# Attention, Mish MLP and bilinear MLP in one kernel: weight conversion in stages, fp32 attention results, a third transpose bank

## The chip, the cores and the metric

The kernel runs on one core of a Trainium2 chip. The metric is the device time of one execution in microseconds (us). Engines are named as the profile names them: PE is TensorE (PEld its weight loads), DVE is VectorE, ACT is ScalarE, POOL is GpSimd, SP is SyncE, whose queue issues the DMAs.

## What is computed

Attention over 4 batches and 8 heads of 576 tokens and 64 dimensions, in which each row keeps only scores within tau of its maximum; then two MLPs over the 2304 tokens.

```python
scores = scale * np.matmul(q, k.transpose(0, 1, 3, 2))
thresh = np.max(scores, axis=-1, keepdims=True) - tau
scores = np.where(scores >= thresh, scores, -1000000000.0)
...
attn = np.exp(scores)
attn = attn / (np.sum(attn, axis=-1, keepdims=True) + 1e-09)
return np.matmul(attn, v).astype(np.float32)
...
h = x @ w_in
sp = np.where(h > 20.0, h, np.log1p(np.exp(np.minimum(h, 20.0))))
g = h * np.tanh(sp)
return (g @ w_out).astype(np.float32)
...
a = x @ w_a
b = x @ w_b
return (a * b @ w_out).astype(np.float32)
```

The model is 512 wide, the first MLP 2048, the second 1536. The weights arrive as 64-bit floats.

## The kernel before

**Attention.** Two heads make a pair, 16 pairs in all. A pair is five units: four of 128 queries for both heads (c = 0 to 3) and one that holds the last 64 queries of both (c = 4, half the columns for DVE and ACT). The loop `for n in range(len(units) + 3)` (L379) takes 80 units through a pipeline of four steps, and the order in which it calls its helpers is, engine by engine, the order in which the engines run (`manual_schedule`). In step n:

- unit n: DVE copies its scores out of PSUM with the row minimum of the negated scores (`least`, L247, one instruction a head); POOL adds the bar (`bars`); ACT takes the exponentials (`expo`, L260).
- unit n-1 (`prev`): DVE masks and sums (`mask`, L265, one a head), POOL adds 1e-9 to the sums (`sums`, L272).
- unit n-2 (`mid`): DVE inverts the sums, POOL spreads the reciprocals into a 128x128 block of `pm` (`spread`, L280), PE transposes `pm` in three parts of 4, 4 and 2 blocks (`turned`, L290) into tiles `tp` of the pool `ps_t`, which has two banks, and ACT copies each part to `pt` (`back`).
- unit n-3 (`old`): PE multiplies with v (`weighted`, L310) into a tile `po` of the pool `ps_o`, which has two banks; DVE multiplies with the transposed reciprocals (`divide`, L324).
- unit n+1: PE computes its scores (`scores`, L233), into the one pair of `sp` tiles there is.

After a pair's last unit, `send` (L335) splits the pair's result into a high and a low fp32r part (ACT, POOL) and writes both to DRAM (`xd`).

**Weights.** PE works in fp32r, so each weight is split in a high and a low part, and each product is three matmuls (`mm3`). A block is a 128x512 piece of a weight. `weight` (L73) converts one in eight stages, each on its engine; from a 64-bit block, the words are put together as: ACT `u` (L94), DVE `a` (L96, L101), POOL add (L105), ACT square (L107), DVE `f` (L109), ACT high part (L111), low part (L113) on the engine that the caller names. `convert(eng)` (L347) goes one stage on where the first block's next stage is on `eng`; the attention loop calls it for ACT, DVE, DVE and POOL in each step from n = 2 on, so a block takes two or three steps, and up to five stages of one block follow each other in one step. All 16 blocks of the first half of w_in and w_out are converted in attention, with the low part on POOL.

**MLPs.** `pipeline` (L460) runs three phases over six tiles of 384 tokens: m1(0) and m1(1), each with half of the 2048 hidden units in eight blocks f, and m2 with twelve. Here the compiler's scheduler orders each engine's work, in the program's order of priority. `load_x` (L144) loads the high and low parts of a tile. The other blocks are converted during the matmuls, with the low part on DVE. PE starts on them while the last attention units are in flight.

Of the kernel before, what the change touches and what calls it, by code (L numbers as in the profile page):

```python
# [21 lines left out]
CC = DM // 128  # L22
# [3 lines left out]
T0 = 2  # L26
# [8 lines left out]
def tile_attn_mish_bilinear(ctx, tc, qd, kd, vd, vd2, tau, w_in, w_out, w_a, w_b, w_out2, out):  # L35
# [23 lines left out]
    xd = [  # L59
        [[dram.tile([128, S], F32, name=f"xd{i}{c}_{b}") for b in range(B)] for c in range(CC)] for i in range(2)  # L60
    ]
# [81 lines left out]

    def load_x(nm, t):  # L144
        x = x_tiles(nm)
        for c in range(CC):
            for i in range(2):
                done = 0
                while done < NM:
                    b, t0 = divmod(t * NM + done, S)  # L150
                    n = min(NM - done, S - t0)
                    nc.sync.dma_start(out=f32(x[c][i][:, done:done + n]), in_=xd[i][c][b][:, t0:t0 + n])
                    done += n
        return x
# [22 lines left out]
    with late_pools:  # L177
        at = late_pools.enter_context(tc.tile_pool(name="at", bufs=1, side="right"))
        ps_t = late_pools.enter_context(tc.tile_pool(name="ps_t", bufs=2, space=PSUM, side="right"))
        ps_o = late_pools.enter_context(tc.tile_pool(name="ps_o", bufs=2, space=PSUM, side="right"))  # L180
# [36 lines left out]
        ph = at.tile([128, 6, 128], F32, name="ph")  # L217

        def new_unit(n):
            pi, c = units[n]  # L220
            nm = f"{pi}_{c}"
            st = lambda s: at.tile([128, 2], F32, tag=s, name=s + nm, bufs=4)
            u = {s: st(s) for s in ("m", "te", "sm", "r")}
            h = 2 if c < 4 else 1
            u.update(pi=pi, c=c, nm=nm, h=h, po=None)
# [46 lines left out]
        def sums(u):  # L272
            n = u["h"]
            G.tensor_scalar(out=u["sm"][:, :n], in0=u["sm"][:, :n], scalar1=1e-9, scalar2=None, op0=ALU.add)
# [5 lines left out]
        def spread(u):  # L280

            if u["h"] == 1:
                G.tensor_copy(u["pm"][:, 5], u["r"][:, :1].to_broadcast([128, 128]))
            else:
                G.tensor_copy(
                    u["pm"][:, 9].rearrange("p (a d) -> p a d", a=2),
                    u["r"].unsqueeze(2).to_broadcast([128, 2, D]),
                )
# [21 lines left out]
        def weighted(u, v):  # L310

            c, pt = u["c"], u["pt"]
            u["po"] = po = ps_o.tile([128, 128], F32, tag="po", name="po" + u["nm"])
# [33 lines left out]
        def convert(eng):  # L347

            if not conv or ahead[0] is not eng:
                return  # L350
            try:
                ahead[0] = next(conv[0])
            except StopIteration:
                conv.pop(0)
                ahead.pop(0)
                if len(conv) > 1:
                    ahead.append(next(conv[1]))

        def attention():
# [7 lines left out]
            ahead.extend(next(g) for g in conv[:2])  # L367
            us = {0: new_unit(0)}
            scores(us[0], data[0])
            late = {}  # L370

            def turn(i):

                u = us[i]
                if u["h"] == 2:
                    return [lambda j=j, m=m: turned(u, j, m) for j, m in ((0, 4), (4, 4), (8, 2))]
                return [lambda j=j, m=m: turned(u, j, m) for j, m in ((0, 4), (4, 2))]

            for n in range(len(units) + 3):  # L379
# [12 lines left out]
                if mid:  # L392
                    parts = turn(n - 2)
                    backs = [part() for part in parts[:-1]]
# [8 lines left out]
                if u and u["h"] == 2:  # L403
                    expo(u, 1)
# [27 lines left out]
            while conv:  # L432
                convert(ahead[0])
# [63 lines left out]
    def m1(half):  # L497
        f0 = half * FC1 // 2

        def first(t, f, x):  # L500
# [4 lines left out]
            return mish(hp, nm)  # L505
# [11 lines left out]
        def after(t, f):  # L517
# [12 lines left out]
            start=lambda t: load_x(f"m{half}_{t}", t), finish=finish, after=after, skew=3,  # L530
# [78 lines left out]
```

## Time and profile before

| | us |
|---|---|
| median of three runs | 1218.99 (1218.48 to 1219.94) |
| the profiled execution's own time | 1222.38 |
| its span, first to last instruction | 1220.6 |
| attention alone: until the first MLP matmul | 354 |
| from there to the end of the span | 867 |

The span lies inside the profiled execution's own time; 1.8 us lie around it. In the views, "busy" is the time in which an engine had an instruction running. On the lines of the timeline, the bracket at the end is the idle time of the engine just before the instruction and what ended it.

### The profile page before, as it was taken

The numbers are of one execution on the slowest core, as the hardware profiler recorded it, in microseconds if no ns is written. First come the engines' busy times: TensorE is split into PE (matmuls) and PEld (weight loads), VectorE is DVE, ScalarE is ACT, GpSimd is POOL, SyncE is SP. The second block draws the span as 40 slices with busy tenths as digits, with TensorE's granted clock in tenths as the row PEclk, the third lists the DMA queues.
The fourth block names the chain that finished last, engine by engine and source line by source line (L and its number), as shares of the span: only waits on it lengthen the run. The fifth ranks groups of instructions, "written<-read, shape, count | busy, mean of one in ns | idle before, by whom it ended". The sixth has DMA issues, their size and how long they took to land.

```text
span 1220.6 us, 20246 instructions
## 1 busy us (share of the span) xinstructions
PE 1170.3 (96%) x7836; PEld 1083.1 (89%) x7836; DVE 585.0 (48%) x1300; ACT 537.0 (44%) x1031; POOL 255.9 (21%) x346
## 2 busy tenths in 40 slices
PE   8888888899999999999999999899999999999998
PEld 5665655677789999999999999899999999999998
DVE  5877778787866991177621138722112121121111
ACT  5777667687865762256522235522112121121211
POOL 2545445465533340022200002200000000000000
PEclk8989899899999999999999999999999999999999
DMA  4334533524304652146533215401001010010000
GB/s 174 119 128 154 175 112 130 181 89 141 120 22 159 214 168 92 53 155 207 190 104 99 83 51 180 151 1 52 1 1 53 1 52 1 1 52 1 26 2 26
DMA packets 75073, 113.53 MB, mean 93 GB/s; under 512 B 6752, under 2 KB 59104, under 8 KB 74976
## 3 DMA queue, kind: packets, MB, share of 16 engines
q1 hardware_dynamic: 74688, 111.93, 27.7%
q8 instruction: 62, 1.02, 0.3%
q10 hardware_dynamic: 288, 0.30, 0.1%
q14 instruction: 35, 0.29, 0.1%
HBM read 88.61 MB, written 23.59 MB: 92 GB/s over the span
## 4 chain that ended last, share of the span: by engine, by line
PE 81%; DVE 10%; ACT 4%; issue 2%; DMA 1%; POOL 1%; SPq 0%; ACTq 0%; DVEq 0%; POOLq 0%
PE acc L134 9%; PE acc L135 9%; PE acc L136 9%; PE po L318 5%; PE hm L134 5%; PE hm L135 5%; PE hm L136 5%; PE tp L303 5%; PE sp L243 4%; PE ha L134 4%; PE ha L135 4%; PE ha L136 4%; PE hb L134 4%; PE hb L136 4%; PE hb L135 4%; DVE s L251 3%
## 5 line engine op out<-in xcount | busy, mean ns | idle before, releaser
L541 DVE TENSOR_TENSOR s<-hb,s 128x384 f32<-128x384 f32 x72 | 40.1, 556 | 275.9 <-PE hb L136 275.9
L105 POOL TENSOR_TENSOR aw<-aw,uw 128x512 int32<-128x512 int32 x68 | 97.6, 1436 | 355.6 <-DVE aw L101 318.0
L173 DVE TENSOR_TENSOR glm<-hsm,ghm 128x384 fp32r<-128x384 f32 x96 | 78.7, 819 | 164.0 <-ACT ghm L172 163.7
L303 PE MATMUL tp<-ident,pm 128*128 128x128 f32 x640 | 105.6, 289 | 34.9 <-DVE pm L266 21.1
L303 PEld LDWEIGHTS tp<-ident,pm 128*128 128x128 f32 x640 | 71.8, 144 | 75.0 <-issue 31.2
L135 PE MATMUL hm<-xlm,w 128*128 128x384 f32 x384 | 129.2, 336 | 0.0
L306 ACT ACTIVATE pt<-tp 128x512 f32<-128x512 f32 (+1 forms) x192 | 98.8, 520 | 68.7 <-PE tp L303 66.4
L134 PE MATMUL hm<-xhm,w 128*128 128x384 f32 x384 | 128.9, 336 | 0.0
L136 PE MATMUL hm<-xhm,w 128*128 128x384 f32 x384 | 128.8, 335 | 0.0
L136 PE MATMUL acc<-ghm,w 128*128 128x384 f32 x384 | 128.7, 335 | 0.0
L135 PE MATMUL acc<-glm,w 128*128 128x384 f32 x384 | 128.7, 335 | 0.0
L134 PE MATMUL acc<-ghm,w 128*128 128x384 f32 x384 | 128.7, 335 | 0.0
L251 DVE TENSOR_SCALAR_CACHE_REDUCE s<-sp 128x576 f32<-128x576 f32 x144 | 103.9, 754 | 31.3 <-PE sp L243 22.9
L540 ACT ACTIVATE s<-ha 128x384 f32<-128x384 f32 x72 | 35.3, 490 | 187.1 <-PE ha L136 187.1
L171 ACT ACTIVATE hsm<-hm 128x384 f32<-128x384 f32 x96 | 46.7, 486 | 153.6 <-PE hm L136 153.3
L263 ACT ACTIVATE ex<-s,m 128x576 f32<-128x576 f32 x144 | 109.2, 769 | 8.3 <-DVE s L251 7.3
L266 DVE SCALAR_TENSOR_TENSOR pm<-s,te,ex 128x576 f32<-128x576 f32 x128 | 105.0, 857 | 0.0
L134 PE MATMUL acc<-gh,w 128*128 128x384 f32 x288 | 96.7, 337 | 4.2 <-DVE y L512 2.5
L135 PE MATMUL acc<-gl,w 128*128 128x384 f32 x288 | 97.1, 337 | 0.5 <-DVE gl L71 0.5
L134 PE MATMUL ha<-xhy,w 128*128 128x384 f32 x288 | 97.0, 337 | 0.0
L135 PE MATMUL ha<-xly,w 128*128 128x384 f32 x288 | 96.9, 336 | 0.0
L136 PE MATMUL ha<-xhy,w 128*128 128x384 f32 x288 | 96.8, 336 | 0.0
(80 smaller groups left out, 2482.3 us busy)
## 6 DMA issues: line engine op xcount, KB each, us to landing
raww<-w_out SPq DMA_DIRECT2D x28, 512.0 KB, 4.1
v<-vd SPq DMA_DIRECT2D x16, 576.0 KB, 4.3
raww<-w_in SPq DMA_DIRECT2D x16, 512.0 KB, 4.3
xhm<-xd SPq DMA_DIRECT2D x32, 192.0 KB, 4.0
xlm<-xd SPq DMA_DIRECT2D x32, 192.0 KB, 4.1
raww<-w_a SPq DMA_DIRECT2D x12, 512.0 KB, 3.6
raww<-w_b SPq DMA_DIRECT2D x12, 512.0 KB, 3.9
v<-vd SPq DMA_DIRECT2D x16, 320.0 KB, 4.7
```

Source lines behind the costliest of these rows:

```text
L105: G.tensor_tensor(out=a, in0=a, in1=u, op=ALU.add)
L134: PE.matmul(ps, wh, xh, start=start, stop=False)
L135: PE.matmul(ps, wh, xl, start=False, stop=False)
L136: PE.matmul(ps, wl, xh, start=False, stop=stop)
L173: V.tensor_tensor(out=g[1], in0=hs, in1=f32(g[0]), op=ALU.subtract)
L243: PE.matmul(sp[:, half, 0:288], d["qs"][r, cols], d["k"][r, keys], start=True, stop=True)
L251: V.tensor_scalar(out=u["s"][:, h].rearrange("p (a c) -> p a c", a=2), in0=u["sp"][h][:, :, 0:288], scalar1=1.0, scalar2=None, op0=ALU.mul ...
L263: A.activation(u["e"][:, h], u["s"][:, h], AF.Exp, bias=u["m"][:, h:h + 1], scale=-1.0)
L266: V.scalar_tensor_tensor(out=u["pm"].rearrange("p a c -> p (a c)")[:, h * S:(h + 1) * S], in0=u["s"][:, h], scalar=u["te"][:, h:h + 1], in ...
L303: PE.transpose(tp[:, i], pm[:, j0 + i], ident)
L306: A.activation(pt[:, j0:j0 + m], tp[:, :m], AF.Copy)
L318: PE.matmul(po[r], v[0][:, j + 4 * h, r], pt[:, j + 4 * h], start=j == 0, stop=j == 4)
```

## The change

- **Conversion.** `convert` no longer looks for an engine. It is called once a step, and a block goes on by one stage a step (the POOL add and the ACT square in one), so that what a stage reads was issued a step earlier. A new block starts every eight steps (`PACE`). Ten blocks (`EARLY` = 5, twice) are converted in attention, the low part on DVE; the other six of the first half in m1(0), tile 0.
- **Attention results** leave as one fp32 array `xd`; `load_x` loads that and splits it (ACT, DVE). The first tile is loaded and split during the last four pairs (`first_x`).
- **POOL** keeps `bars` and the conversion's add. `sums` goes to DVE, `spread` to ACT.
- **PSUM.** `ps_t` has three banks; `ps_o` has one, `sums_o`, whose four 128-column slots the units take in turn.
- **Order in a step.** `invert` stands ahead of the transposes, the second `expo` behind the scores of the next unit.

```diff
-T0 = 2
+T0, PACE, EARLY = 1, 8, 5
...
+    x0 = x_tiles("first")
...
     def load_x(nm, t):
         x = x_tiles(nm)
         for c in range(CC):
-            for i in range(2):
-                done = 0
-                while done < NM:
...
-                    nc.sync.dma_start(out=f32(x[c][i][:, done:done + n]), in_=xd[i][c][b][:, t0:t0 + n])
+            raw = mp.tile([128, NM], F32, tag="ys", name=f"xr{nm}_{c}", bufs=4)
+            fetch_x(raw, c, t)
+            split(*x[c], raw, V)
         return x
...
-        ps_t = late_pools.enter_context(tc.tile_pool(name="ps_t", bufs=2, space=PSUM, side="right"))
-        ps_o = late_pools.enter_context(tc.tile_pool(name="ps_o", bufs=2, space=PSUM, side="right"))
+        ps_t = late_pools.enter_context(tc.tile_pool(name="ps_t", bufs=3, space=PSUM, side="right"))
+        ps_o = late_pools.enter_context(tc.tile_pool(name="ps_o", bufs=1, space=PSUM, side="right"))
...
+        sums_o = ps_o.tile([128, 4, 128], F32, name="sums_o")
...
         def sums(u):
-            G.tensor_scalar(out=u["sm"][:, :n], in0=u["sm"][:, :n], scalar1=1e-9, scalar2=None, op0=ALU.add)
+            V.tensor_scalar(out=u["sm"][:, :n], in0=u["sm"][:, :n], scalar1=1e-9, scalar2=None, op0=ALU.add)
...
         def spread(u):
-                G.tensor_copy(
+                A.activation(
                     u["pm"][:, 9].rearrange("p (a d) -> p a d", a=2),
-                    u["r"].unsqueeze(2).to_broadcast([128, 2, D]),
+                    u["r"].unsqueeze(2).to_broadcast([128, 2, D]), AF.Copy,
                 )
...
         def weighted(u, v):
-            u["po"] = po = ps_o.tile([128, 128], F32, tag="po", name="po" + u["nm"])
+            u["po"] = po = sums_o[:, u["n"] % 4]
...
         def send(pi):
-            hi, lo = (at.tile([128, S], F32R, tag="ax" + s, name=f"ax{s}{pi}", bufs=2) for s in "hl")
-            out = xs["u"]
-            split(hi, lo, out, G)
             b, p = pairs[pi]
-            for i, part in enumerate((hi, lo)):
-                nc.sync.dma_start(out=xd[i][p][b], in_=f32(part))
+            nc.sync.dma_start(out=xd[p][b], in_=xs["u"])
+
+        def first_x(c, load):
+            if load:
+                xs["raw"] = at.tile([128, NM], F32, tag="xr", name=f"xr{c}", bufs=1)
+                fetch_x(xs["raw"], c, 0)
+            else:
+                split(*x0[c], xs["raw"], V)
 
-        conv = [w1_stages(f, i, wa_p, WA, G) for f in range(FC1 // 2) for i in range(2)]
-        ahead = []
-        def convert(eng):
-            if not conv or ahead[0] is not eng:
-                return
-            try:
-                ahead[0] = next(conv[0])
-            except StopIteration:
...
+        conv = [w1_stages(f, i, wa_p, WA, V) for f in range(EARLY) for i in range(2)]
+        GROUPS = (0, 1, 1, 1, 2, 1, 1, 1)
+        active = []
+        def convert(start):
+            for item in list(active):
+                stages, k = item
+                for _ in range(GROUPS[k]):
+                    if next(stages, None) is None:
+                        active.remove(item)
+                        break
+                item[1] += 1
+            if start and conv:
+                active.append([conv.pop(0), 0])
+                next(active[-1][0])
...
                 if mid:
+                    invert(mid)
...
                     backs[0]()
                 if u:
                     expo(u, 0)
                 if mid:
-                    invert(mid)
                     spread(mid)
...
-                if u and u["h"] == 2:
-                    expo(u, 1)
                 if old:
                     weighted(old, vs[old["pi"]])
                 if n + 1 < len(units):
...
                 if mid:
-                    back = parts[-1]()
-                if u:
-                    if c == 3 and pi + 1 < len(pairs):
-                        scale_q(data[pi + 1], slice(0, 640))
-                    if n >= T0:
-                        convert(A)
-                        convert(V)
+                    back = turned(mid, *parts[-1])
+                if u and u["h"] == 2:
+                    expo(u, 1)
+                if u and c == 3 and pi + 1 < len(pairs):
+                    scale_q(data[pi + 1], slice(0, 640))
+                convert(T0 <= n < len(units) and (n - T0) % PACE == 0)
...
-                if u and n >= T0:
-                    convert(V)
-                    convert(G)
+                if u and pi >= len(pairs) - CC and c in (0, 2):
+                    first_x(pi - len(pairs) + CC, c == 0)
...
-            return mish(hp, nm)
+            parts = mish(hp, nm)
+            if half == 0 and t == 0 and EARLY + f < FC1 // 2:
+                load_w1(EARLY + f, wa_p, WA, V)
+            return parts
...
-            start=lambda t: load_x(f"m{half}_{t}", t), finish=finish, after=after, skew=3,
+            start=lambda t: load_x(f"m{half}_{t}", t) if t or half else x0, finish=finish, after=after, skew=3,
```

How the order moves, at two places. In the names, pm3_2 is the masked block of pair 3, unit 2, and fw12_1 the tile `f` of w_out's third block (the number at the end counts tiles).

First place: the stage `f` of that block. Before, ACT in the step of unit 3_3:

```order
L306 ACTIVATE pt3_1_1058<-tp3_1_4_1205 128x512
L263 ACTIVATE ex3_3_1211<-s3_3_1196,m3_3_1161 128x576
L201 ACTIVATE qs4_1018<-qr4_1016,nsc_76 128x640
L107 ACTIVATE fw12_1_960<-raww12_1_956 128x512
L306 ACTIVATE pt3_1_1058<-tp3_1_8_1236 128x256
```

and DVE in the same step:

```order
L251 TENSOR_SCALAR s3_3_1196,m3_3_1161<-sp3_3_1_1168 128x576
L278 RECIPROCAL r3_1_1056<-sm3_1_1055 128x2
L109 SCALAR_TENSOR_TENSOR fw12_1_960<-fw12_1_960,aw12_1_959 128x512
L266 SCALAR_TENSOR_TENSOR pm3_2_1104,sm3_2_1102<-s3_2_1129,te3_2_1101,ex3_2_1144 128x576 x2
L330 TENSOR_TENSOR u3_1245<-po3_0_1217,pt3_0_997 128x128
```

DVE's L109 reads what ACT's L107 writes in that step, late in ACT's row, and the masks stand behind it. In the change ACT has the square in the step of unit 9_1:

```order
L268 ACTIVATE ex9_1_2596<-s9_1_2585,m9_1_2564 128x576
L105 ACTIVATE fw12_1_2365<-raww12_1_2361 128x512
L304 ACTIVATE pth8_4_2463<-tp8_4_4_2621 64x128
L305 ACTIVATE pth8_4_2463<-tp8_4_4_2621 128x128
L311 ACTIVATE pt9_0_2513<-tp9_0_0_2638 128x512
L268 ACTIVATE ex9_2_2649<-s9_2_2633,m9_2_2609 128x576
L290 ACTIVATE pm9_0_2512<-r9_0_2511 128x128
```

and DVE its use in the step of unit 9_2:

```order
L271 SCALAR_TENSOR_TENSOR pm9_0_2512,sm9_0_2510<-s9_0_2534,te9_0_2509,ex9_0_2550 128x576 x2
L279 TENSOR_SCALAR sm9_0_2510<-sm9_0_2510 128x2
L335 TENSOR_TENSOR u8_2476<-sums_o_172,pt8_3_2407 128x128
L256 TENSOR_SCALAR s9_2_2633,m9_2_2609<-sp9_2_1_2616 128x576
L283 RECIPROCAL r9_0_2511<-sm9_0_2510 128x2
L107 SCALAR_TENSOR_TENSOR fw12_1_2365<-fw12_1_2365,aw12_1_2364 128x512
L271 SCALAR_TENSOR_TENSOR pm9_1_2568,sm9_1_2566<-s9_1_2585,te9_1_2565,ex9_1_2596 128x576 x2
```

A whole step now lies between the two, with ACT's spread (L290) and DVE's sums (L279) new in the rows. Second place: PE around a unit's product with v, with the engines that each row waits for. Before:

```order
L318 MATMUL po3_1_1267<-pt3_1_1058,v3_900 64x128 x10
L243 MATMUL sp4_0_0_1284<-k4_1017,qs4_1018 128x288 [waits DMAHW7_49]
L243 MATMUL sp4_0_1_1285<-k4_1017,qs4_1018 128x288 [waits DVE_49]
L303 MATMUL tp3_2_8_1290<-ident_69,pm3_2_1104 128x128 [waits Activation_49]
L303 MATMUL tp3_3_0_1315<-ident_69,pm3_3_1165 128x128 [waits DVE_49,Activation_49]
L303 MATMUL tp3_3_4_1320<-ident_69,pm3_3_1165 128x128 [waits DVE_49,Activation_49]
```

and in the change:

```order
L308 MATMUL tp4_2_0_1422<-ident_69,pm4_2_1290 128x128 [waits DVE_49,PE_49]
L308 MATMUL tp4_2_4_1427<-ident_69,pm4_2_1290 128x128 [waits DVE_49,Activation_49]
L323 MATMUL sums_o_172<-pt4_1_1246,v4_1103 64x128 [waits DVE_49]
L323 MATMUL sums_o_172<-pt4_1_1246,v4_1103 64x128 x8
L323 MATMUL sums_o_172<-pt4_1_1246,v4_1103 64x128 [waits Activation_49]
L248 MATMUL sp5_0_0_1453<-k5_1207,qs5_1208 128x288 [waits DMAHW5_49]
```

The product waited for no other engine at its start; now its first matmul waits for DVE, whose division of the unit before reads the same bank, and its last for ACT's copy of the third part. Over the whole program, SP issues 64 loads and 16 stores of `xd` where it issued 128 and 32.

## Rows read from the trace of the kernel before

**Rows 1.** The page, part 1: busy us, share of the span, instructions.

```profile
PE 1170.3 (96%) x7836; PEld 1083.1 (89%) x7836; DVE 585.0 (48%) x1300; ACT 537.0 (44%) x1031; POOL 255.9 (21%) x346
```

**Rows 2.** Busy time by stretch (start:end, length, engines, granted clock, DMA share, GB/s).

```profile
core 0: us, PE busy (x) PEld busy (x) DVE busy (x) ACT busy (x) POOL busy (x), PEclk, DMA share, GB/s
142.42:214.32 71.90, 60.40 (x548) 43.65 (x547) 54.43 (x156) 50.93 (x94) 36.46 (x58) 0.93 0.40 135
258.21:350.36 92.15, 90.87 (x912) 66.92 (x911) 76.12 (x236) 70.75 (x131) 47.82 (x81) 1.00 0.32 111
354.00:1220.60 866.60, 857.86 (x4978) 855.36 (x4974) 313.22 (x500) 283.01 (x569) 77.61 (x56) 1.00 0.24 77
390.00:420.00 30.00, 30.00 (x175) 30.00 (x174) 26.73 (x37) 21.67 (x41) 11.82 (x8) 1.00 0.59 185
```

**Rows 3.** Timeline of PE: scores of unit 4 of the first and last pair.

```profile
18.51 1.24 PE L245 MATMUL sp<-k,qs 128*128 128x288 f32 x4
...
350.29 1.24 PE L245 MATMUL sp<-k,qs 128*128 128x288 f32 x4
```

**Rows 4.** Waits of DVE, 10 to 258: total us, times, longest.

```profile
DVE fw L109 <- ACT fw L107: 35.0, 16, 2.6
```

**Rows 5.** Timeline around one conversion stage: start, duration, instruction, idle time before it.

```profile
164.48 0.82 ACT L201 ACTIVATE qs<-qr,nsc 128x640 f32<-128x640 f32 x1
...
165.20 0.65 ACT L107 ACTIVATE fw<-raww 128x512 f32<-128x512 f32 x1
...
165.96 0.69 DVE L109 SCALAR_TENSOR_TENSOR fw<-fw,aw 128x512 f32<-128x512 f32 x1 [2.64 <-ACT fw L107]
...
167.53 0.63 PE L303 MATMUL tp<-ident,pm 128*128 128x128 f32 x4 [2.16 <-DVE pm L266]
```

**Rows 6.** The chain of waits in attention: start, us, what.

```profile
140.09 2.33 PE po L318 x20
...
253.42 0.88 PE po L320 x20
...
295.05 1.17 PE sp L245 x4
...
301.48 1.24 PE po L318 x20
302.72 1.17 PE sp L243 x8
303.89 0.81 PE tp L303 x6
```

**Rows 7.** Timeline, a part of four transposes, its weight loads.

```profile
300.82 0.42 PEld L303 LDWEIGHTS tp<-ident,pm 128*128 128x128 f32 x4 [0.27 <-ACT pt L306]
```

**Rows 8.** Timeline of DVE: two small dependent instructions at the start.

```profile
3.34 0.16 DVE L54 TENSOR_TENSOR bar<-tau_t,big 128x1 f32<-128x1 f32 x1
3.53 0.17 DVE L56 COPY bar<-bar 128x2 f32<-128x2 f32 x1
```

**Rows 9.** Groups by line and shape: count, busy us, mean ns, idle before.

```profile
L96 DVE TENSOR_SCALAR aw<-raww 128x512 int32<-128x512 int32 x68 | 30.6, 450 | 6.8 <-DMA raww<-w_b 2.9 <-DMA raww<-w_in 2.5
L101 DVE SCALAR_TENSOR_TENSOR aw<-raww,aw 128x512 int32<-128x512 int32 x68 | 46.9, 689 | 1.4
L109 DVE SCALAR_TENSOR_TENSOR fw<-fw,aw 128x512 f32<-128x512 f32 x68 | 46.7, 687 | 56.5 <-ACT fw L107 45.8 <-POOL aw L105 10.7
L113 DVE TENSOR_TENSOR w<-fw,w 128x512 fp32r<-128x512 f32 x52 | 46.6, 896 | 3.0 <-ACT w L111 3.0
L300 ACT ACTIVATE pth<-tp 128x128 f32<-128x128 f32 x16 | 4.1, 258 | 0.0
L70 ACT ACTIVATE xhy<-yr 128x384 fp32r<-128x384 f32 x24 | 12.3, 527 | 15.9 <-DMA yr<-y1d 15.9
```

**Rows 10.** Timeline of DVE under the MLP's matmuls, two blocks' low parts.

```profile
753.63 1.78 DVE L113 TENSOR_TENSOR w<-fw,w 128x512 fp32r<-128x512 f32 x1
...
758.49 1.78 DVE L113 TENSOR_TENSOR w<-fw,w 128x512 fp32r<-128x512 f32 x1
```

More of the change, by code (lines that the diff above doesn't have):

```diff
@@ L58, in tile_attn_mish_bilinear @@
     w1 = [[None, None] for _ in range(FC1)]
-    xd = [
-        [[dram.tile([128, S], F32, name=f"xd{i}{c}_{b}") for b in range(B)] for c in range(CC)] for i in range(2)
-    ]
+    xd = [[dram.tile([128, S], F32, name=f"xd{c}_{b}") for b in range(B)] for c in range(CC)]
     y1d, ypd = (
@@ L142, in x_tiles, with fetch_x @@
         ]
+    x0 = x_tiles("first")
+    def fetch_x(raw, c, t):
+        done = 0
+        while done < NM:
+            b, t0 = divmod(t * NM + done, S)
+            n = min(NM - done, S - t0)
+            nc.sync.dma_start(out=raw[:, done:done + n], in_=xd[c][b][:, t0:t0 + n])
+            done += n
     def load_x(nm, t):
@@ L146, in load_x @@
         for c in range(CC):
-            for i in range(2):
-                done = 0
-                while done < NM:
-                    b, t0 = divmod(t * NM + done, S)
-                    n = min(NM - done, S - t0)
-                    nc.sync.dma_start(out=f32(x[c][i][:, done:done + n]), in_=xd[i][c][b][:, t0:t0 + n])
-                    done += n
+            raw = mp.tile([128, NM], F32, tag="ys", name=f"xr{nm}_{c}", bufs=4)
+            fetch_x(raw, c, t)
+            split(*x[c], raw, V)
         return x
@@ L224, in new_unit @@
             h = 2 if c < 4 else 1
-            u.update(pi=pi, c=c, nm=nm, h=h, po=None)
+            u.update(n=n, pi=pi, c=c, nm=nm, h=h, po=None)
             u["pm"] = at.tile([128, 10, 128], F32, tag="pm", name="pm" + nm, bufs=3) if h == 2 else ph
@@ L282, in spread @@
             if u["h"] == 1:
-                G.tensor_copy(u["pm"][:, 5], u["r"][:, :1].to_broadcast([128, 128]))
+                A.activation(u["pm"][:, 5], u["r"][:, :1].to_broadcast([128, 128]), AF.Copy)
             else:
-                G.tensor_copy(
+                A.activation(
                     u["pm"][:, 9].rearrange("p (a d) -> p a d", a=2),
-                    u["r"].unsqueeze(2).to_broadcast([128, 2, D]),
+                    u["r"].unsqueeze(2).to_broadcast([128, 2, D]), AF.Copy,
                 )
@@ L335, in send @@
         def send(pi):
-            hi, lo = (at.tile([128, S], F32R, tag="ax" + s, name=f"ax{s}{pi}", bufs=2) for s in "hl")
-            out = xs["u"]
-            split(hi, lo, out, G)
             b, p = pairs[pi]
-            for i, part in enumerate((hi, lo)):
-                nc.sync.dma_start(out=xd[i][p][b], in_=f32(part))
-        conv = [w1_stages(f, i, wa_p, WA, G) for f in range(FC1 // 2) for i in range(2)]
-        ahead = []
-        def convert(eng):
-            if not conv or ahead[0] is not eng:
-                return
-            try:
-                ahead[0] = next(conv[0])
-            except StopIteration:
[L354 to L357, printed above, removed]
+            nc.sync.dma_start(out=xd[p][b], in_=xs["u"])
[19 more added lines that the diff above has]
+                next(active[-1][0])
         def attention():
@@ L366, in attention @@
             vs[0] = load_v(0)
-            ahead.extend(next(g) for g in conv[:2])
             us = {0: new_unit(0)}
             scores(us[0], data[0])
[L370 to L377, printed above, removed]
             for n in range(len(units) + 3):
@@ L392, in attention @@
                 if mid:
-                    parts = turn(n - 2)
-                    backs = [part() for part in parts[:-1]]
+                    invert(mid)
+                    parts = ((0, 4), (4, 4), (8, 2)) if mid["h"] == 2 else ((0, 4), (4, 2))
+                    backs = [turned(mid, j, m) for j, m in parts[:-1]]
                     backs[0]()
@@ L425, in attention @@
                         send(old["pi"])
-                if u and n >= T0:
-                    convert(V)
-                    convert(G)
+                if u and pi >= len(pairs) - CC and c in (0, 2):
+                    first_x(pi - len(pairs) + CC, c == 0)
                 if mid:
                     back()
-            while conv:
-                convert(ahead[0])
         with tc.manual_schedule():
```

## The prediction

> **What bounds the kernel now.** The busy times come first [rows 1]: PE is busy for 96% of the span, and no other engine for half of it. That is an average over stages, so the stretches come next [rows 2]. From 354 us on, in the MLPs, PE is busy for 857.86 of 866.60 us: that stage is at PE's limit, and only a longer wait could change it. Attention fills the 354 us before, and it runs at two paces. Between 258.21 and 350.36, five pairs without conversion take 92.15 us, 18.43 each, with PE busy for 90.87. Between 142.42 and 214.32, three pairs with conversion take 71.90 us, 23.97 each, with PE busy for 60.40 at a granted clock of 0.93. The scores of unit 4 mark the pairs: from the first pair's to the last's, 331.78 us pass in 15 pairs, 22.12 us a pair [rows 3].
>
> The waits say what the slow pairs wait for. DVE's `f` stage waited 16 times for ACT's square, 35.0 us in all [rows 4]. The timeline shows how [rows 5]: ACT does the scaling of q first (0.82 us), then the square (0.65); DVE, which takes its instructions in order, stands idle for 2.64 us in front of L109 with two masks behind it; PE then waits 2.16 us for the first mask. After such a gap PE also runs slower: twenty passes of a product take 2.33 us at 140.09 and 1.24 at 301.48 [rows 6].
>
> **The wait inside conversion.** By the order, an instruction of a block now reads what was issued a step earlier, so the 35.0 us go, with the slow clock behind them. What is late next are PE and DVE themselves, so I add up both for a pair of the new kernel.
>
> **PE, per pair.** A double unit costs 1.24 for its product and 1.17 for its scores [rows 6]. Six transposes and the change-over take 0.81 [rows 6], and a transpose 0.42 / 4 = 0.105 [rows 7], so its ten take 0.81 + 4 x 0.105 = 1.23. That makes 3.64. The fifth unit costs 0.88 + 1.17 + 0.81 = 2.86 [rows 6]. Sum: 4 x 3.64 + 2.86 = 17.42 us. The 1.0 us up to 18.43 is mostly the wait of a transpose part for its bank (0.27 before one part [rows 7]); the third bank takes that away.
>
> **DVE, per pair.** 76.12 / 5 = 15.22 us now [rows 2]. Five `sums` come from POOL; no DVE row shows one. From below they cost nothing, where DVE idles anyway; from above, the 0.19 us from one small dependent instruction's start to the next's [rows 8], 0.95 a pair, which I take, since they too wait for a result just made. Ten blocks at 0.450 + 0.689 + 0.687 + 0.896 = 2.72 us [rows 9] over 16 pairs are 1.70. Sum: 17.87 us. The low part is the uncertain one of the four: 0.896 is a mean, and beside POOL's add it took 1.78 [rows 10].
>
> **ACT, per pair.** 70.75 / 5 = 14.15 now [rows 2]. Five `spread` come from POOL: between 0.258 us (a 128x128 copy out of PSUM) and 0.527 (384 columns from SBUF) [rows 9]; I take 0.3, 1.5 a pair. Conversion adds three stages of about 0.65 [rows 5], 1.2 a pair. The split of the result goes. About 16.5 us, under the other two, so ACT's share is covered; without that cover the spreads would cost 1.5 a pair.
>
> **Pace.** DVE's 17.87 and PE's 17.42 stand side by side and hand work to each other, so the pace lies at or above the larger. Conversion falls into half of the steps, which then run longer on DVE, while in the two steps where DVE has a single head PE is the longer. I take 18.2, a third of a microsecond above DVE. Bounds: 17.42, if DVE overlaps more than its busy time says, and 20.08, below. Gain: 15 x (22.12 - 18.2) = 58.8 us.
>
> **The other parts.** The six blocks that move out of attention come one every 4.86 us under the MLP's matmuls [rows 10], so the first, third and fifth (w_in for f = 5, 6, 7) are there after 4.9, 14.6 and 24.3 us. A matmul takes 30 / 175 = 0.171 us [rows 2]. By PE's order it has 60 matmuls to do before the first, 48 more before the third and 31 more before the fifth: 10.3, 18.5 and 23.8 us, and the last units' 26 transposes and four products (2.7 + 4.6 us [rows 6, 7]) stand among them. PE is covered with some 7 us to spare; without the cover, rival C. Loading x in fp32 halves SP's loads and stores of `xd`, in which PE waits for nothing now; its 44 splits in the MLPs (0.527 on ACT [rows 9], about as much on DVE) lie beside matmuls where DVE is busy for 313 of 867 us and ACT for 283 [rows 2]. The first tile's splits fall into four of 80 steps, 2 us of each engine. I put 1 us on these parts together, bounds 0 and 5. POOL's lighter load I count at nothing. SP moves nothing past a wait that PE feels.
>
> **Sum.** -58.8 + 1 = -57.8 us. The profiled execution took 1222.38 us (its span 1220.6), 3.4 above the median; a difference between two paces carries over, so 1222.38 becomes 1164.6 and the median of 1218.99 becomes **1161**.
>
> **Rivals.** *A: one bank for the products locks PE to DVE.* A product's first matmul now waits for DVE's division of the unit before, the last work of DVE's step, so PE cannot work ahead, and what is added to DVE's step could come on top of PE's: 17.42 + 0.95 + 1.70 = 20.08 a pair, 15 x 2.04 = 30.6 us gained, 1189. For it: the order's new wait. Against it: PE does a product and the next scores, 2.4 us, while DVE does the step's row minima and masks, so it can start late. [...] No row here shows one bank.
>
> *B: conversion still costs what it did.* Blocks cost (331.78 - 15 x 18.43) / 16 = 3.46 us each over the clean pace [rows 2 to 4]. If the cost is the work and not the wait, ten blocks on the clean pace give 276.5 + 34.6 = 311.1 us instead of 331.8, with the 1 us 1199: the change would not do what it says. For it: DVE's and ACT's work of a block is the same. Against it: 35.0 of the 55.3 us are that one wait.
>
> *C: the six late blocks hold PE up.* If, among the last masks and copies, a block takes twice 4.86 us, the fifth is there after 48.6 us against the 31 that PE has: 17.5 us, 1178.
>
> *D: slower.* Small gaps in every step could keep PE's clock down through attention: at the rate of the 2.33 us row [rows 6] PE's 17.42 become nearly twice that. From a share of 0.27 of attention at the low level on (17.42 x 1.27 = 22.12, a mean granted clock of about 0.86), the kernel is slower than now; with half, 26.1 a pair, 60 us more, 1279. For it: 0.93 in the slow pairs. Against it: 1.00 in the clean ones [rows 2], whose gaps the new pace resembles. [...]
>
> **How the numbers follow.** Forecast 0.64, A 0.15, B 0.09, C 0.07, D 0.04, no change 0.01. About 0.2% (2.4 us) is what a measurement can tell from no change. Faster: all but the last two, 0.95. The forecast's own range runs from PE's bound, 15 x 4.70 = 70.5 us gained, 1148, up to about 1175. B, D and a little at the low end are left out (under 0.2); A ends the range at 1189.
>
> **What would show it.** Right: the wait of DVE's `f` for ACT is gone; the marks of unit 4 come every 18 us or so; DVE and PE are both busy for over nine tenths of attention at a clock near 1.00; the first MLP matmul starts near 295. A shows as PE waiting for the division before a product; C as PE waiting for `w` after 295; B as marks 20 us apart or more. The forecast is wrong if the marks stay over 19.5 us or the MLPs take over 872.

## The result and the profile after

The changed kernel takes 1171.27 us (median of four runs, 1168.02 to 1171.47) against 1219.47: a ratio of 0.9597, 95% interval 0.9578 to 0.9617. Its profiled execution took 1171.47 us (span 1169.6), so span against span the change is -51.0 us. The forecast was 1161 with a range of 1148 to 1189, and -57.8 us between the profiled executions: faster as forecast, 10 us less so.

The page's part 1, answering to [rows 1]:

```profile
PE 1148.9 (98%) x7836; PEld 1075.7 (92%) x7836; DVE 636.3 (54%) x1444; ACT 563.3 (48%) x1143; POOL 152.8 (13%) x154
```

Busy time by stretch, as in [rows 2]: ten pairs with conversion, the last four pairs (conversion, and the split of the first tile of x), and the MLPs from their first matmul on:

```profile
core 0: us, PE busy (x) PEld busy (x) DVE busy (x) ACT busy (x) POOL busy (x), PEclk, DMA share, GB/s
38.42:217.96 179.54, 177.11 (x1823) 135.25 (x1821) 171.42 (x546) 157.11 (x320) 41.04 (x56) 1.00 0.36 124
217.96:292.62 74.66, 71.38 (x731) 54.15 (x729) 69.12 (x223) 62.93 (x131) 15.11 (x22) 1.00 0.36 124
297.42:1169.60 872.18, 860.87 (x4977) 856.82 (x4976) 363.60 (x581) 313.98 (x639) 86.49 (x59) 1.00 0.23 72
```

In the ten pairs PE is busy for 177.11 of 179.54 us and DVE for 171.42, at a granted clock of 1.00; before, three such pairs had PE busy for 60.40 of 71.90 at 0.93 [rows 2]. The timeline of PE: scores of unit 4 of the first and last pair, as in [rows 3], and the first MLP matmul:

```profile
20.22 1.24 PE L250 MATMUL sp<-k,qs 128*128 128x288 f32 x4
...
292.62 1.24 PE L250 MATMUL sp<-k,qs 128*128 128x288 f32 x4
...
297.42 0.44 PE L132 MATMUL hm<-xhfirst,w 128*128 128x384 f32 x1
```

(292.62 - 20.22) / 15 is 18.16 us a pair; before it was 22.12, and 18.2 was forecast. So the span's 51.0 us are: 15 pairs x 3.96 = 59.4 gained; 1.7 lost before the first mark (20.22 against 18.51); 1.0 from the last mark to the first MLP matmul (4.80 against 3.76); 5.6 in the MLPs (872.18 against 866.55). The pace came as forecast. The 8.4 us beside it stood in the forecast as 1, and 872.18 us in the MLPs is, by 0.2 us, one of the prediction's own signs of being wrong ("the MLPs take over 872").

DVE's waits between 12 and 297 us, where [rows 4] had 35.0 us (the two with most and least of a list of four):

```profile
DVE s L256 <- PE sp L248: 11.0, 21, 1.6
...
DVE w L111 <- ACT w L109: 0.2, 1, 0.2
```

The stage `f` (now L107) is not in the list. DVE now waits for PE's scores, that is, for the engine that is busy for 177.11 of 179.54 us in the ten pairs. PE's waits in the ten pairs are small, and two of three are the new one, for the division:

```profile
PE sums_o L323 <- DVE u L335: 0.6, 1, 0.6
PE sums_o L323 <- DVE u L338: 0.6, 1, 0.6
PE tp L308 <- DVE pm L271: 0.4, 1, 0.4
```

Where the loss in the MLPs lies, PE's timeline shows (start, duration, instruction, idle time before it):

```profile
318.25 0.41 PE L132 MATMUL acc<-ghm,w 128*128 128x384 f32 x1 [1.11 <-DVE u L338]
...
518.78 0.44 PE L132 MATMUL acc<-ghm,w 128*128 128x384 f32 x1 [2.51 <-ACT y L512]
...
729.88 0.45 PE L132 MATMUL acc<-gh,w 128*128 128x384 f32 x1 [3.43 <-DVE y L510]
```

Before, there were waits of 2.45, 1.79 and 0.54 us around 778 to 793, in place of the third; the first two are new, with one of 0.36 us at 416. Of the 5.6 us, 2.6 are idle time of PE (11.3 of the stretch against 8.7), and the other 3.0 are longer busy time (860.87 against 857.86). After the second of these gaps PE was also slower for a while: from 520 to 530 the granted clock was 0.84 (0.50 up to 523, 1.00 from 524 on), and 51 matmuls ran, where 59 ran in the next 10 us at 1.00. After the third it was 0.83 from 730 to 740, with 49 matmuls; after the first it was 1.00 from 320 to 330, with 60.

### The profile page after: what moved, and what is told of

The parts are those of the page before. It is cut to its first block, busy times and chain, and to the rows that moved or that the text cites. A ratio compares the mean times of both kernels' runs of the same rounds, so it can differ in the third digit from the quotient of the medians.

```text
span 1169.6 us, 20070 instructions
## 1 busy us (share of the span) xinstructions
PE 1148.9 (98%) x7836; PEld 1075.7 (92%) x7836; DVE 636.3 (54%) x1444; ACT 563.3 (48%) x1143; POOL 152.8 (13%) x154
## 4 chain that ended last, share of the span: by engine, by line
PE 74%; DVE 11%; ACT 6%; DMA 4%; issue 4%; POOL 1%; SPq 0%; ACTq 0%; DVEq 0%; POOLq 0%
PE acc L132 8%; PE acc L134 7%; PE acc L133 7%; PE sp L248 6%; PE tp L308 5%; PE sums_o L323 5%; PE hb L132 4%; PE hb L134 4%; PE hb L133 4%; PE ha L132 4%; PE ha L134 4%; PE ha L133 4%; PE hm L133 3%; PE hm L134 3%; PE hm L132 3%
## 5 line engine op out<-in xcount | busy, mean ns | idle before, releaser
L103 POOL TENSOR_TENSOR aw<-aw,uw 128x512 int32<-128x512 int32 x68 | 103.9, 1527 | 361.9 <-DVE aw L99 328.8
L177 DVE TENSOR_TENSOR glm<-hsm,ghm 128x384 fp32r<-128x384 f32 x96 | 74.9, 780 | 109.9 <-ACT ghm L176 109.8
L133 PE MATMUL hm<-xlm,w 128*128 128x384 f32 x352 | 118.3, 336 | 0.0
L134 PE MATMUL hm<-xhm,w 128*128 128x384 f32 x352 | 118.2, 336 | 0.0
L132 PE MATMUL hm<-xhm,w 128*128 128x384 f32 x352 | 118.1, 336 | 0.0
L256 DVE TENSOR_SCALAR_CACHE_REDUCE s<-sp 128x576 f32<-128x576 f32 x144 | 103.6, 752 | 16.5 <-PE sp L248 15.5
L132 PE MATMUL acc<-gh,w 128*128 128x384 f32 x288 | 96.9, 338 | 3.4 <-DVE y L510 3.4
L68 ACT ACTIVATE gh<-s 128x384 fp32r<-128x384 f32 x72 | 37.7, 523 | 127.2 <-DVE s L539 127.2
L271 DVE SCALAR_TENSOR_TENSOR pm<-s,te,ex 128x576 f32<-128x576 f32 x128 | 98.9, 809 | 0.0
L134 PE MATMUL acc<-gh,w 128*128 128x384 f32 x288 | 96.8, 337 | 0.0
```

The lines of the kernel that those rows point to most:

```text
L103: G.tensor_tensor(out=a, in0=a, in1=u, op=ALU.add)
L132: PE.matmul(ps, wh, xh, start=start, stop=False)
L133: PE.matmul(ps, wh, xl, start=False, stop=False)
L134: PE.matmul(ps, wl, xh, start=False, stop=stop)
L177: V.tensor_tensor(out=g[1], in0=hs, in1=f32(g[0]), op=ALU.subtract)
L256: V.tensor_scalar(out=u["s"][:, h].rearrange("p (a c) -> p a c", a=2), in0=u["sp"][h][:, :, 0:288], scalar1=1.0, scalar2=None, op0=ALU.mul ...
```

## The experiments

Ratios are to the kernel before, which took 1218.2 to 1219.3 us in these runs. The change's own four runs span 3.5 us, so differences of some 2 us from it tell nothing.

**1. One stage moved back.** The edit lets DVE's `f` follow ACT's square, and GpSimd's add that `f` reads too, in the same step; the two stages after it come a step earlier, and all else is the change.

```diff
-        GROUPS = (0, 1, 1, 1, 2, 1, 1, 1)
+        GROUPS = (0, 1, 1, 1, 3, 1, 1)
```

> The changed kernel with one stage moved: DVE's f stage of a block is issued in the same step as ACT's square that it reads, as in the kernel before. Theory 1 (the gain is the wait that went): the wait of DVE fw L107 for ACT fw L105 comes back 10 times with some 2 us each, PE behind it slows down, so 10 blocks cost 2.2 to 3.46 us more each: 22 to 35 us, the time is 1193 to 1206 us, the marks of unit 4 come every 19.6 to 20.5 us. Theory 2 (the gain is lighter POOL, fp32 results, the third bank): no wait of more than 3 us in all, 1171 us within 3.

Measured: 1195.13 us (0.9801, 0.9787 to 0.9814), 23.9 slower than the change; 19.58 us a pair. The groups by line from 25 to 290 us show the wait again:

```profile
L107 DVE SCALAR_TENSOR_TENSOR fw<-fw,aw 128x512 f32<-128x512 f32 x9 | 6.2, 692 | 20.4 <-ACT fw L105 20.4
```

9 waits of 2.27 us, and PE in the same stretch at 0.97 with 17.3 us of waits for masks behind them (13.9 and, in fifth units, 3.4). One step between writer and reader is worth half of the whole change. Theory 1 holds: of the two results that `f` reads, the square is the one that the waits are put down to.

**2. All 16 blocks in attention.**

```diff
-T0, PACE, EARLY = 1, 8, 5
+T0, PACE, EARLY = 1, 4, 8
```

> The changed kernel with all 16 blocks of the first half converted in attention, one started every 4 steps; no block moves to the MLPs. Theory 1 (the 5.6 us that the MLPs lost in the changed kernel come from the six late blocks, which fill DVE and ACT from 297 us on and push the conversions behind them up to the phase boundary at 516): the waits of acc at 318 and 518 us go, from the first MLP matmul to the end 866 to 868 us instead of 872; attention pays between 0 and 15 us for six more blocks on DVE. Time 1165 to 1181. Theory 2 (the splits of the fp32 x on ACT and DVE cause them): MLPs stay at 871 to 873 us, the wait at 518 stays.

Measured: 1178.97 us (0.9673, 0.9660 to 0.9686); 19.13 us a pair; MLPs 868.40. DVE now has no room left, from 25 to 290 us:

```profile
25.00:290.00 265.00, 251.52 (x2506) 187.63 (x2505) 259.25 (x785) 229.47 (x467) 69.66 (x87) 1.00 0.39 130
```

The six blocks cost 0.97 us a pair, 14.6 us, and give back 3.8 us in the MLPs, where the wait at 318 us is gone; the one at the phase boundary stays (2.56 us at 528). So the late blocks explain a part of the MLPs' loss and not the boundary's wait. Theory 2's splits of x are taken up below.

**3. Four blocks in attention**, twelve behind it.

```diff
-T0, PACE, EARLY = 1, 8, 5
+T0, PACE, EARLY = 1, 8, 2
```

> The changed kernel with 4 blocks instead of 10 converted in attention (they end with pair 8), 12 moved under the first tile of the first MLP. What it measures is the pace of the new attention without conversion. Theory 1 (a staged block costs next to nothing): pairs without blocks take 17.9 to 18.2 us, as with them. Theory 2 (DVE sets the pace, its work of a block counts): pairs without blocks take 16.5 to 17.5 us. For the late blocks: the first tile now needs a block every 2.05 us where one is made in 4.86, so the MLPs take 30 to 50 us longer and the time is 1195 to 1225; if they are covered, 1165 to 1175.

Measured: 1177.24 us (one run), MLPs 866.64. The expected loss in the MLPs did not come: the compiler's scheduler put the blocks that are written behind attention into it, 13 `f` stages from 128 to 235 us, in pairs of 20.9 to 22.4 us. The last four pairs have no block:

```profile
235.26:305.06 69.80, 69.74 (x730) 53.72 (x728) 63.47 (x210) 58.83 (x124) 14.05 (x20) 1.00 0.33 110
```

17.45 us a pair, theory 2's number (16.5 to 17.5), but with PE busy throughout: it is PE's own sum, forecast as 17.42, that sets it, and not DVE's. What a block costs depends on what stands beside it. Against the 17.95 of the change's ten pairs with 0.625 blocks each it is 0.8 us; but these last four pairs also hold the first tile's splits, and against the change's last four, which have both (18.67), it is 2.0. Before, it was 3.46.

**4. The staging alone**, in the kernel before: its `convert` replaced by that of the change, 16 blocks, one started every 4 steps, low part on GpSimd.

```diff
-                    if n >= T0:
-                        convert(A)
-                        convert(V)
+                convert(T0 <= n < len(units) and (n - T0) % 4 == 0)
...
-                if u and n >= T0:
-                    convert(V)
-                    convert(G)
```

> The kernel before with the staged conversion alone: 16 blocks, one started every 4 steps, low part still on GpSimd, all else as before. Theory 1 (the wait is what mattered): the wait of DVE's f stage for ACT's square goes (35.0 us before), pairs come every 18.4 to 19.5 us, 1165 to 1185 us. Theory 2 (the other parts of the change matter more): 1205 to 1222 us.

Measured: 1179.06 us (0.9672, 0.9659 to 0.9685); 19.32 us a pair. The waits from 10 to 300 us, of DVE and of PE:

```profile
DVE fw L109 <- ACT fw L107: 1.3, 1, 1.3
...
PE tp L303 <- ACT pt L306: 11.2, 14, 1.4
```

35.0 us of DVE's waiting for the square are 1.3, and 40 of the 48 us are there. What is late next are the transposes, for one of their two banks.

**5. The banks as before**: two for the transposes, two for the products.

```diff
-        ps_t = late_pools.enter_context(tc.tile_pool(name="ps_t", bufs=3, space=PSUM, side="right"))
-        ps_o = late_pools.enter_context(tc.tile_pool(name="ps_o", bufs=1, space=PSUM, side="right"))
+        ps_t = late_pools.enter_context(tc.tile_pool(name="ps_t", bufs=2, space=PSUM, side="right"))
+        ps_o = late_pools.enter_context(tc.tile_pool(name="ps_o", bufs=2, space=PSUM, side="right"))
...
-            u["po"] = po = sums_o[:, u["n"] % 4]
+            u["po"] = po = ps_o.tile([128, 128], F32, tag="po", name="po" + u["nm"])
```

> The changed kernel with the PSUM of the kernel before: two banks for the transposes, two for the products. Rival A (one product bank locks PE to DVE): the marks come closer than 18.16 us, PE's waits for the division go, 1155 to 1168 us. The prediction's view (a third transpose bank removes PE's waits for ACT's copies; the one product bank costs little): the waits of a transpose for ACT's copy of pt come back, as in the staged-only kernel, where they were 11.2 us; 0.2 to 0.9 us a pair, 1174 to 1185 us.

Measured: 1183.02 us (0.9712, 0.9692 to 0.9732), 11.7 slower than the change; 19.16 us a pair. From 25 to 290 us PE's first wait is

```profile
PE tp L307 <- ACT pt L310: 8.4, 12, 1.5
```

In the change PE has no such wait. The third bank is worth more than the second product bank; what each is worth by itself no run separates. Rival A falls.

**6. Staging with the change's spacing** in the kernel before: experiment 4 with ten blocks, one every 8 steps, and `load_w1` for the other six as in the change.

```diff
-                convert(T0 <= n < len(units) and (n - T0) % 4 == 0)
+                convert(T0 <= n < len(units) and (n - T0) % 8 == 0)
```

> The kernel before with the staged conversion and its spacing of the change: ten blocks, one every 8 steps, six blocks in the first tile of the MLP; low part in attention on GpSimd, all else as before. If the staging and the spacing make the whole gain, 1168 to 1174 us; if the other parts (third bank, sums and spread off GpSimd, fp32 results) carry the rest, pairs take 18.7 to 19.0 us and the time is 1176 to 1183 us.

Measured: 1176.87 us (0.9660, 0.9644 to 0.9676); 18.96 us a pair. Six blocks less bring 2.2 us (1.5 by the ratios, within their intervals), and the rest of the change 5.6: the second case. The rest is more than the banks: experiment 5, which has it all but them, is 6.2 us slower than this kernel. So without the third bank the other parts (`sums` and `spread` moved, the low part on DVE, fp32 results, the order in a step) together cost time; fp32 results in attention and the order in a step were not tried alone.

**7. The low part on GpSimd.**

```diff
-        conv = [w1_stages(f, i, wa_p, WA, V) for f in range(EARLY) for i in range(2)]
+        conv = [w1_stages(f, i, wa_p, WA, G) for f in range(EARLY) for i in range(2)]
```

> The changed kernel with the low part of the ten blocks on GpSimd instead of DVE. If DVE's sum sets the pace (95% busy in attention), 0.625 blocks a pair times 0.68 us leave it: marks every 17.6 to 17.9 us instead of 18.16, 1162 to 1168 us. If PE's sum or the handing over sets it, 1169 to 1172 us; if GpSimd's work beside DVE slows DVE, 1173 or more.

Measured: 1173.47 us (0.9626, 0.9605 to 0.9646), no gain; 18.24 us a pair. Of the expected cases the third fits: from 25 to 290 us DVE lost nine low parts of 0.68 us and was as busy as in the change, 250.8 of 265 us. The groups by line say why, this kernel's first:

```profile
L279 DVE TENSOR_SCALAR sm<-sm 128x2 f32<-128x2 f32 x57 | 22.9, 402 | 2.0
...
L111 POOL TENSOR_TENSOR w<-fw,w 128x512 fp32r<-128x512 f32 x9 | 15.6, 1729 | 0.0
```

and the changed kernel's:

```profile
L279 DVE TENSOR_SCALAR sm<-sm 128x2 f32<-128x2 f32 x57 | 16.3, 287 | 2.0
```

`sums`, two numbers a partition, grew by 6.6 us in all, what the low parts had saved. The timeline of the changed kernel shows how:

```profile
146.99 1.86 POOL L103 TENSOR_TENSOR aw<-aw,uw 128x512 int32<-128x512 int32 x1
...
147.76 1.12 DVE L279 TENSOR_SCALAR sm<-sm 128x2 f32<-128x2 f32 x1
148.79 0.28 DVE L335 TENSOR_TENSOR u<-sums_o,pt 128x128 f32<-128x128 f32 x1
...
149.12 1.31 PE L323 MATMUL sums_o<-pt,v 128*64 128x128 f32 x20 [0.63 <-DVE u L335]
...
151.92 0.17 DVE L279 TENSOR_SCALAR sm<-sm 128x2 f32<-128x2 f32 x1
```

GpSimd's add ends at 148.85, DVE's `sums` at 148.88: it does not end before the add does, and takes 1.12 us instead of 0.17. The division behind it comes late, and PE's next product waits for it. So it is with eight of the change's ten adds in attention: each time `sums` takes 1.12 us, some 7.6 us too much in all; with the low parts on GpSimd it is fifteen times. Beside the other two adds a `sums` on one number a partition, started 0.02 us behind the add, took 0.15 us and ended over a microsecond before it. What holds the eight up, and whether it is the two numbers or the start 0.77 us into the add that sets them apart from the other two, no run shows.

**8. `sums` and `spread` back on GpSimd.**

```diff
-            V.tensor_scalar(out=u["sm"][:, :n], in0=u["sm"][:, :n], scalar1=1e-9, scalar2=None, op0=ALU.add)
+            G.tensor_scalar(out=u["sm"][:, :n], in0=u["sm"][:, :n], scalar1=1e-9, scalar2=None, op0=ALU.add)
...
-                A.activation(
+                G.tensor_copy(
                     u["pm"][:, 9].rearrange("p (a d) -> p a d", a=2),
-                    u["r"].unsqueeze(2).to_broadcast([128, 2, D]), AF.Copy,
+                    u["r"].unsqueeze(2).to_broadcast([128, 2, D]),
                 )
```

> The changed kernel with sums and spread back on GpSimd. DVE loses 0.29 us a unit, 1.45 a pair. If DVE's sum sets the pace: marks every 17.5 to 17.8 us, 1161 to 1167 us. If the chain through GpSimd (sum, reciprocal, spread, transpose) is what the change was right to shorten: pairs of 18.3 us or more, 1173 to 1185 us, with PE waiting for spread or DVE for sums.

Measured: 1173.22 us (0.9625, 0.9611 to 0.9639). 17.90 us a pair, and the first MLP matmul 5.8 us earlier, at 291.64. But the MLPs took 877.86 us, 5.7 more, with 8.2 us of waits of `acc` for `y`. In attention PE now waits for the spread:

```profile
PE tp L308 <- POOL pm L290: 3.3, 9, 0.9
```

The pace came near the first expected outcome (17.5 to 17.8), and the total fell into the second's range (1173 to 1185), but not for the second's reason: what attention gained the MLPs lost.

**9. A second buffer for `f`.**

```diff
-        tl = lambda s, dt: cv.tile(shape, dt, tag="cv" + s, name=s + name, bufs=1)
+        tl = lambda s, dt: cv.tile(shape, dt, tag="cv" + s, name=s + name, bufs=2 if s == "f" else 1)
```

> The changed kernel with two buffers instead of one for the tile f of a conversion. Theory (in the MLPs ACT's square of the next block waits for DVE's low part, which reads the one f and takes 1.78 us beside GpSimd's add; in ACT's queue the copies y stand behind that square, and PE's acc waits for y): the wait of L105 for L111 (56.6 us, 50 times) goes, the waits of acc for y at 416 and 518 us go, the MLPs take 864 to 868 us instead of 872, 1163 to 1168 us. Rival (the copies are late because of where the compiler's order puts them, whatever f does): MLPs 870 to 876 us, 1169 to 1175. Attention stays at 18.1 to 18.2 us a pair in both.

Measured: 1169.12 us (0.9596, 0.9583 to 0.9609), no difference from the change that can be told (2.2 us); MLPs 873.25. ACT's wait from 290 to 760 us is still

```profile
ACT fw L105 <- DVE w L111: 50.6, 41, 2.5
```

where the change has 56.6 us, 50 times. The waits at 416 and 518 us went and one of 3.46 us came at 385. The wait at the phase boundary is gone from experiments 10 to 12 too, which have the second buffer as well; but the time that the theory forecast for it did not come, and its rival's numbers hold. What stood ahead of the copies at 518 us is in ACT's queue of the changed kernel:

```profile
515.47 0.66 ACT L105 ACTIVATE fw<-raww 128x512 f32<-128x512 f32 x1 [2.34 <-DVE w L111]
516.05 0.67 ACT L92 ACTIVATE uw<-raww 128x512 int32<-128x512 uint32 x1
516.96 0.63 ACT L109 ACTIVATE w<-fw 128x512 fp32r<-128x512 f32 x1 [0.24 <-DVE fw L107]
517.50 0.47 ACT L175 ACTIVATE hsm<-hm 128x384 f32<-128x384 f32 x1
517.87 0.48 ACT L176 ACTIVATE ghm<-hm 128x384 fp32r<-128x384 f32 x1
518.24 1.26 ACT L512 ACTIVATE y<-acc 128x384 f32<-128x384 f32 x3
```

The copies `y`, for which PE stands, are behind three stages of a conversion and a Mish. ACT idles 2.34 us for DVE's low part, which took 1.79 us there beside GpSimd's add instead of 0.68, with the copies behind it.

**10. Experiments 8 and 9 together.**

> The same two buffers for f in the kernel with sums and spread on GpSimd, whose attention ended 5.8 us earlier than that of the changed kernel and whose MLPs took 877.9 us. If the first theory holds: first MLP matmul at 291 to 293 us, MLPs 864 to 868, time 1157 to 1163 us, the fastest so far. If the order of the copies decides whatever f does: MLPs 872 to 878, 1167 to 1173.

Measured: 1165.22 us (0.9560, 0.9546 to 0.9573); first MLP matmul at 291.65, MLPs 871.95. 8.0 us faster than experiment 8 by the medians and 5.9 by the profiled executions, all of the 5.9 in the MLPs, where experiment 9 had gained nothing: between the two expected cases.

**11. `sums` alone on GpSimd**, with two buffers for `f`.

```diff
-            V.tensor_scalar(out=u["sm"][:, :n], in0=u["sm"][:, :n], scalar1=1e-9, scalar2=None, op0=ALU.add)
+            G.tensor_scalar(out=u["sm"][:, :n], in0=u["sm"][:, :n], scalar1=1e-9, scalar2=None, op0=ALU.add)
```

> Two buffers for f, and of the two small steps only sums on GpSimd; spread stays on ACT. If DVE's sums, which run up to 1.5 us beside GpSimd's add, are what the change paid too much for: pairs of 17.6 to 17.9 us and no wait of PE for GpSimd's spread, first MLP matmul at 288 to 292 us. If spread on GpSimd was the better half of that kernel: pairs of 18.0 us or more, first matmul at 293 to 296. MLPs 866 to 876 either way; time 1158 to 1167 in the first case, 1165 to 1172 in the second.

Measured: 1161.93 us (0.9529, 0.9516 to 0.9542), the fastest of all: 7.2 us under experiment 9, from which it differs in that line alone, and 9.3 under the change. 17.67 us a pair, first MLP matmul at 287.89. Its stretch from 25 to 290 us:

```profile
25.00:290.00 265.00, 261.87 (x2722) 201.54 (x2721) 241.73 (x745) 234.27 (x482) 78.23 (x160) 1.00 0.37 123
```

and the changed kernel's:

```profile
25.00:290.00 265.00, 259.28 (x2660) 197.49 (x2661) 250.89 (x796) 229.47 (x469) 59.84 (x82) 1.00 0.35 119
```

DVE is 9.2 us less busy and PE 2.6 more, 99% of the stretch. The first case: `spread` was right to leave GpSimd, `sums` was not. (The longest of the change's 80 `sums` took 1.13 us, not the expectation's 1.5.)

**12. Half of the copies on DVE**, in experiment 10's kernel.

```diff
-                    A.activation(y, acc[c], AF.Copy)
+                    if c % 2:
+                        V.tensor_copy(y, acc[c])
+                    else:
+                        A.activation(y, acc[c], AF.Copy)
```

> sums and spread on GpSimd, two buffers for f, and in the first MLP's first half two of the four copies of acc on DVE instead of ACT. If the waits of acc come from ACT's full queue alone: the wait at 378 us (3.3 us) shrinks below 1.5, MLPs 866 to 870, 1159 to 1163 us. If DVE's queue holds its copies up as long (low parts of 1.78 us in it): acc waits for DVE in its place, MLPs 871 to 876, 1164 to 1169 us.

Measured: 1163.66 us (0.9542, 0.9529 to 0.9555), MLPs 871.32. The wait at 378 us is 2.11 us instead of 3.27, and it is for DVE's copy now. The second case, 0.3 us under its range: either queue holds the copies up. The 1.6 us to experiment 10 lie within the runs of both.

## Why the prediction held, and where it did not

**The wait inside conversion.** Right. One stage back costs 23.9 us (experiment 1); the staging alone gains 40 of the 48 (experiment 4). The 23.9 are a net figure: in experiment 1 no `sums` met an add.

**PE's sum.** Right: 17.42 forecast, 17.45 without blocks (experiment 3). As a bound it is a little high: single pairs of experiment 11 took 17.29. The third bank does take away the transposes' wait: with two and two banks the kernel is 11.7 us slower (experiment 5).

**DVE's sum.** 17.87 forecast, 171.42 / 10 = 17.14 measured. The base held: without `sums` and the conversion's rows DVE's busy time in the ten pairs is 15.14 a pair, 15.22 in the forecast. `sums` add 0.87 to it (0.95 forecast) and the blocks 1.13 (1.70). The step that failed is the block's price, means of rows added to a busy time: neighbours on DVE overlap in the trace (above, the division starts at 148.79 and `sums` ends at 148.88), so that the rows of the ten pairs add up to 207.5 us in 171.42 of busy time. The low part was also shorter in attention, 0.676 us and not 0.896: GpSimd's add, which the forecast feared beside it, met `sums` instead. A `sums`, put at 0.19 us "from above", took 1.12 beside the add: a long GpSimd instruction was left in the very step in which a short one came to DVE. That `sums` on DVE cost 7.2 us experiments 9 and 11 show; that the meetings are the most of it is likely by the 7.6 us above, and no run moves them alone.

**ACT's sum.** 16.5 forecast, 157.11 / 10 = 15.7 measured: covered, as said.

**Pace.** 18.2 forecast, 18.16 measured: 17.95 in the ten pairs and 18.67 in the last four, where the splits of x are added to the blocks. So close a hit is partly luck: DVE's sum was 0.7 too high, the third of a microsecond above the larger sum was 0.53 in the ten pairs (over PE's 17.42), and the splits, which the forecast had among the other parts, cost some 3 us of the 15 pairs. That DVE's work is part of what lies above PE's sum, experiments 2 (more of it, slower) and 11 (less of it, faster) bear out; experiment 2 gives ACT and GpSimd more work too.

**The other parts.** This is the step that failed most: "I put 1 us on these parts together, bounds 0 and 5". It was 8.4.
- 1.7 us at the start: from 10 to 15 us the granted clock was 0.62, and 0.50 from 12 on, in the profiled execution (the third column from the end):

```profile
10.00:15.00 5.00, 4.61 (x17) 3.03 (x16) 4.94 (x17) 1.91 (x3) 1.36 (x2) 0.62 0.74 291
```

Experiment 3's kernel, which is the same up to there, had 1.00:

```profile
10.00:15.00 5.00, 4.56 (x24) 2.57 (x23) 4.11 (x14) 3.04 (x5) 0.90 (x2) 1.00 0.76 296
```

In the kernel before it was 1.00 there too; and the eight transposes that the change begins at 13.39 us took 1.97 us, where the same eight took 1.09 in the kernel before and in experiments 3, 5 and 9 to 12. This part therefore differs from run to run, and no term of the change stands behind it. Nor did the sum's base carry over: the profiled execution of before was 3.4 us above the median, that of after 0.2.
- 1.0 us between the last mark and the MLP: one wait of 0.63 us for the division, and transposes.
- 5.6 us in the MLPs. The forecast asked whether PE would wait for a late block's `w`; it never did, so that cover held. It did not ask who stands behind the late blocks on DVE and ACT: the last division (318 us) and the copies of `acc` (518). With no late blocks to convert there the MLPs took 868.40 and 866.64 us (experiments 2 and 3). The forecast also counted the 44 splits of x as lying beside matmuls. In their MLPs the programs of experiments 2 and 4 differ by them alone: both convert all 16 blocks in attention, and experiment 4 loads x split already. Its MLPs took 863.96 us against 868.40, and the wait at the phase boundary is not there. PE's waits from 300 us on, two of experiment 2's four and experiment 4's only one:

```profile
PE acc L132 <- ACT y L512: 2.6, 1, 2.6
PE acc L132 <- DVE y L510: 2.5, 1, 2.5
...
PE acc L134 <- DVE y L505: 2.6, 1, 2.6
```

  Experiment 6, with late blocks and no splits, took 868.25, the change with both 872.18. By these four profiled executions the late blocks and the splits cost some 4 us each; against the kernel before the loss is 5.6, since its MLPs, without either, took 2.6 us more than experiment 4's. One execution of each is thin ground: kernels with both took 871.3 to 877.9 us (experiments 12 and 8). What in the compiler's order puts a copy ahead of a conversion stage or behind it stays open.

**The rivals.** A: two product banks were slower, and PE's waits for the division between 12 and 297 us came to 2.5 us, 4 times. A's price was 1189; 1171 was measured, with the order's waits between PE and DVE on the one bank. B: a block costs 0.8 to 2.0 us, not 3.46. C: no wait for `w` in the change; in experiments 10 to 12, whose attention ends earlier, there were 0.4 to 1.0 us of it, so the cover is thinner than the forecast's 7 us. D: the granted clock was 1.00 from 25 to 290 us. (D's mean clock of 0.86 is a slip in the prediction: where 17.42 us of work at full clock take 22.12, the mean is 17.42 / 22.12 = 0.79, if PE's time goes with the clock. D's factor of two is an estimate: of the two products in [rows 6] the one at a granted clock of 0.50 took 2.33 / 1.24 = 1.88 times as long as the one at 1.00.)

## What to carry to other kernels

Look for an instruction that reads what another engine writes late in the same step: everything behind it in the order waits with it, and one step of distance was worth 24 us here with the work unchanged. When work is moved between DVE and GpSimd, look at which long instruction of the one runs at the same time as which short one of the other, not only at the sum of busy times; and when means of rows are added to a busy time, remember that rows can overlap (here 207.5 us of rows in 171.42 of busy time). When work is moved off a critical stage into a covered one, ask for every instruction that queues behind it there, not only for its own consumer.

## What was not expected of the hardware

A DVE instruction on 128x2 numbers took 1.12 us instead of 0.17 when GpSimd had a 128x512 add running, and ended 0.02 to 0.03 us after it, eight times of eight. The add itself took 1.86 or 1.87 us there, with one of DVE's masks still running as it began, and 1.27 beside the other two `sums`, where a mask had just ended and DVE idled for 0.83 and 0.72 us of it. And the same beginning of the program ran once at a granted clock of 0.62 and once at 1.00 (from 10 to 15 us, the change and experiment 3).
